# Local attention over key groups of 64, PSUM as eight freely placed banks, and a planner that charges mode changes

## The chip, the cores and the metric

The kernel runs on one core of one Trainium2 chip. Times are device microseconds of that core. Two kernels are compared by runs of the same rounds on the same chip. A run is "fast" or "slow", a slow one being over 1.5% above the fastest of its kernel. Engines are named as in the profile: PE is the matmul engine, PEld its weight loads, ACT the scalar engine, DVE the vector engine, POOL the third compute engine, SP the one that issues DMAs (in the kernel before all but one, of 0.9 KB).

## The reference, cut to what matters

```python
def _A_ref(x, wqkv, wo):               # S=2048 tokens, D=448, H=16 heads of 28
    W, dil = (8, 2)                    # each query sees 8 keys, every second position back
    ...
    logits = einsum('bhsd,bhswd->bhsw', q, kg) * scale
    attn = _softmax(where(mask, logits, -1e9))
    o = einsum('bhsw,bhswd->bhsd', attn, vg)
    return o.transpose(...).reshape(B, S, D) @ wo

x = x + ga * _A_ref(layernorm(x) * (1 + ca) + sa, A_wqkv, A_wo)
x = x + gb * _B_ref(layernorm(x) * (1 + cb) + sb, ...)     # an MLP 448 -> 1792 -> 448
```

The kernel keeps even and odd positions apart, so that the dilated window becomes 8 neighbours.

## The kernel before

A planner in Python adds tasks with a duration, an engine, dependencies and buffers. It simulates the engines and fixes the order of instructions on each engine and the buffer each task gets. The framework derives the semaphores afterwards. Two constants of the old planner: PSUM is `"L": 2` tiles of two banks and `"S": 4` tiles of one bank.

```python
def ps_big(shape, name):
    return Buf("L", lambda k: ps.tile(shape, FP32, name=name, tag=f"L{k}"), name)
def ps_one(shape, name, dtype=FP32):
    return Buf("S", lambda k: ps.tile(shape, dtype, name=name, tag=f"S{k}"), name)
```

Attention goes in 17 blocks of 121 queries against 128 keys. 16 logit matmuls use four row tiles of the array at a time; the denominators and the outputs use four column tiles. In the trace of this kernel the four logit matmuls of a round start within 11 ns, and the rounds of a group 52 to 66 ns apart (median 56).

```python
def lmm():
    for ft in range(4):
        for r in range(4):
            nc.tensor.matmul(lts[r // 2].t[:, r % 2, ft * EQ:(ft + 1) * EQ],
                             lhsT=kT[HP * r:HP * r + DH, ft, k0:k0 + BK],
                             rhs=qT[HP * r:HP * r + DH, ft, q0:q0 + EQ],
                             start=True, stop=True, tile_position=(HP * r, 0))
lm = add("PE", 0.45, lmm, ...)
...                                     # exp on ACT, mask on DVE
def dmm():
    for r in range(4):                  # denominators: 4 matmuls of 488 columns
        ...
    for ft in range(4):
        for r in range(4):              # outputs: 16 matmuls of 121 columns
            ...
add("PE", 0.62, dmm, ...)
```

The softmax here doesn't subtract the row's maximum and nothing guards it: scores larger than these inputs give would overflow.

Of the kernel before, what the change touches and what calls it, by code (L numbers as in the profile page):

```python
# [25 lines left out]
BQ, BK, EQ = 121, 128, 122  # L26
NBA = 17
WT = LEAD + SL + SEP + SL + 4
OTW = 9 * BQ
# [5 lines left out]
PASSES = (44,)  # L35
# [4 lines left out]
    (range(0, 5), [0]),  # L40
    (range(5, 9), [1, 2]),
    (range(9, 14), [3, 4]),
    (range(14, 17), [5, 6, 7]),
]
FILL_UNTIL, FILL_SHARE = 12.0, 1.0
ROOM = {"L": 2, "S": 4, "et": 3, "den": 4, "zh": 6, "yT": 3, "hm": 3, "vb": 3}
# [4 lines left out]
class Buf:  # L51


    def __init__(self, room, make, name=""):
        self.room, self.make, self.name, self.users, self._t = room, make, name, [], None
        self.slot = None
# [8 lines left out]
class Task:  # L65
    def __init__(self, n, eng, us, fn, bufs, rank_add, late, dense, port):
        self.n, self.eng, self.us, self.fn, self.bufs = n, eng, us, fn, bufs
        self.name = f"{eng} {fn.__qualname__.split('.')[-1]}:{fn.__code__.co_firstlineno}"
        self.rank_add, self.late, self.dense, self.port = rank_add, late, dense, port
        self.before, self.after = {}, []  # L70
        self.rank = 0.0
        self.fill = 0


class Planner:
# [6 lines left out]
    def add(self, eng, us, fn, reads=(), writes=(), bufs=(), after=(), order_after=(), rank_add=0.0, late=0.0, dense=1.0, port=False):  # L82
        t = Task(len(self.tasks), eng, us, fn, bufs, rank_add, late, dense, port or eng == "POOL")
# [59 lines left out]

    def forward(self):
# [6 lines left out]
        room = {r: [0.0] * n for r, n in ROOM.items()}  # L151
        users_left = {b: len(b.users) for t in self.tasks for b in t.bufs}
        free_at = {e: START for e in DRAIN}
        order = []
        now = START
        port = {"DVE": 0.0, "POOL": 0.0}
        while len(order) < len(self.tasks):
            started = False
            for e in ("PE", "DVE", "ACT", "POOL", "SP"):
                if free_at[e] > now:  # L160
                    continue
                best = None
                shared = e in port and port["DVE" if e == "POOL" else "POOL"] > now
                for t in ready[e]:
                    if ready_at[t] > now or (shared and t.port) or (best is not None and (t.rank, -t.n) < (best.rank, -best.n)):
                        continue
                    need = {}
                    for b in t.bufs:
                        if b.slot is None:
                            need[b.room] = need.get(b.room, 0) + 1  # L170
                    if all(sum(x <= now for x in room[r]) >= n for r, n in need.items()):
                        best = t
# [10 lines left out]
                for b in t.bufs:  # L183
                    if b.slot is None:
                        b.slot = min(range(ROOM[b.room]), key=lambda k: room[b.room][k])
                        room[b.room][b.slot] = 1e9
                end = now + t.us
                free_at[e] = end
# [3 lines left out]
                for b in t.bufs:  # L192
                    users_left[b] -= 1
                    if users_left[b] == 0:
                        room[b.room][b.slot] = done + SEM
# [10 lines left out]
            times = [v for v in free_at.values() if v > now] + [v for r in room.values() for v in r if now < v < 1e9]  # L206
            times += [ready_at[t] for e in ready for t in ready[e] if ready_at[t] > now]
# [24 lines left out]
    def plan(self):  # L232
        self.ranks()
        base = {t: t.rank for t in self.tasks}
        best, self.log = (None, None, 1e9), []
        for seed in PASSES:
            rnd = random.Random(seed)
            for t in self.tasks:
                t.rank = base[t] * (1.0 + (NOISE * rnd.gauss(0.0, 1.0) if seed else 0.0))
            for again in range(3):  # L240
                self.clear()
                order, span = self.forward()
# [3 lines left out]
                self.log.append((round(span, 1), round(cost, 1), seed))  # L246
                if cost < best[2]:
                    best = ([(t, t.fill) for t in order], {b: b.slot for t in order for b in t.bufs}, cost)
                self.backward()
        self.order, slots, self.span = best  # L250
        for b, k in slots.items():
            b.slot = k
# [9 lines left out]
def kernel(  # L262
# [28 lines left out]
    def ps_big(shape, name):  # L291
        return Buf("L", lambda k: ps.tile(shape, FP32, name=name, tag=f"L{k}"), name)

    def ps_one(shape, name, dtype=FP32):
        return Buf("S", lambda k: ps.tile(shape, dtype, name=name, tag=f"S{k}"), name)
# [22 lines left out]
    mask = cst.tile([128, 8, EQ], BF16, name="mask")  # L318
    ones_k = cst.tile([128, 3, HP], BF16, name="ones_k")
    neg_half = cst.tile([128, 4], FP32, name="neg_half")  # L320
    eps_col = cst.tile([128, 1], FP32, name="eps_col")
# [14 lines left out]
    NX1P = 8  # L336
    NZ, NY, NV = 4, 4, 3
# [110 lines left out]
    pool(0.1, lambda: nc.gpsimd.memset(neg_half[:], -0.5), ["neg_half"])  # L448
    pads = [(0, LEAD), (LEAD + SL, LEAD + SL + SEP), (LEAD + 2 * SL + SEP, WT)]
    for (a, b) in pads:  # L450
        for i, tl in enumerate((hT, kT, qT)):
            pool(0.12, lambda a=a, b=b, tl=tl: nc.gpsimd.memset(tl[:, :, a:b], 0.0), [f"pad{i}{a}"])
    PADK = [f"pad{i}{a}" for i in range(3) for (a, _) in pads]
    pool(0.9, lambda: nc.gpsimd.memset(mask[:], 1.0), ["mask"])
    pool(1.0, lambda: nc.gpsimd.affine_select(out=mask[:], in_=mask[:], pattern=[[0, 8], [1, EQ]],
                                              compare_op=ALU.is_ge, fill=0.0, base=WIN - 1, channel_multiplier=-1),
         ["mask"])
    pool(1.0, lambda: nc.gpsimd.affine_select(out=mask[:], in_=mask[:], pattern=[[0, 8], [-1, EQ]],
                                              compare_op=ALU.is_ge, fill=0.0, base=0, channel_multiplier=1), ["mask"])

    def consts():
# [4 lines left out]
        nc.gpsimd.memset(ones_k[64:64 + WIN - 1, 2, :], 0.0)  # L466
# [10 lines left out]
    pwm = ps_big([128, 2, 512], "pwm")  # L477
# [46 lines left out]
    P.wrote(add("PE", 0.3, c_cols, reads=["c_row", "c_tail", "one1"], bufs=[psc]), psc)  # L524
# [26 lines left out]
    def evac_h(kt, ptr, k, c0, n, eng, bs):  # L551
        kw = KE[kt]
# [11 lines left out]
    def front_ln(bs, on_act):  # L564
# [10 lines left out]
        for half, eng in enumerate(("DVE", "ACT")):  # L575
# [9 lines left out]
            P.wrote(add("PE", 0.13 * n, tr, reads=["ident", "ztail"] + [f"z{b % NZ}" for b in bs], bufs=[ptr]), ptr)  # L585
# [22 lines left out]
    def front_qk(bs, engs, bonus=0.0):  # L608
        n, c0 = 128 * len(bs), tok_col(bs[0])
        for m in range(8):  # L610
# [7 lines left out]
            P.wrote(add("PE", 4 * n / 2400 + 0.02, mm,  # L618
# [11 lines left out]
    def mods():  # L630
# [9 lines left out]
        P.wrote(add("PE", 1.1, mm, rank_add=150, reads=["silu_bc"] + [f"wmod2{i}{h}" for i in range(2) for h in "ab"] + ["wmod00", "wmod01"],  # L640
# [26 lines left out]
    def attention(b, tbl, prev_w1):  # L667
        q0 = LEAD + b * BQ
        k0 = q0 - (WIN - 1)
        tb = blocks_of(b * BQ - (WIN - 1), b * BQ + EQ)  # L670
        vbuf = Buf("vb", lambda k: vbufs[k], "vb")
        pv = ps_one([128, D], "pv")

        def vmm():
            for kt in range(KT):
                nc.tensor.matmul(pv.t[:], lhsT=hT[0:KE[kt], kt, k0:k0 + BK], rhs=Wv[0:KE[kt], kt, :],  # L676
                                 start=(kt == 0), stop=(kt == KT - 1))

        P.wrote(add("PE", 0.76, vmm, reads=["wva", "wvb", "Wv0"] + PADK + [f"h{kt}_{t}" for kt in range(KT) for t in tb], bufs=[pv, vbuf]), pv)
        P.wrote(add("ACT", 0.45, lambda: nc.scalar.copy(out=vbuf.t[:, :, 0:DH],  # L680
                                                        in_=pv.t[:].rearrange("p (h d) -> p h d", h=H)),
                    bufs=[pv, vbuf], reads=["vpad"]), vbuf)
        et = sb("et", [128, 4, 4, EQ], BF16, "et")
        lts = [ps_big([128, 2, 512], "lt") for _ in range(2)]

        def lmm():
            for ft in range(4):
                for r in range(4):
                    nc.tensor.matmul(lts[r // 2].t[:, r % 2, ft * EQ:(ft + 1) * EQ],  # L689
                                     lhsT=kT[HP * r:HP * r + DH, ft, k0:k0 + BK],  # L690
                                     rhs=qT[HP * r:HP * r + DH, ft, q0:q0 + EQ],
                                     start=True, stop=True, tile_position=(HP * r, 0))

        lm = add("PE", 0.45, lmm, dense=0.1, reads=PADK + [f"{s}{ft}_{t}" for s in "qk" for ft in range(4) for t in tb],
                 bufs=lts, order_after=prev_w1)
        P.wrote(lm, *lts)
        lt_mms.append(lm)
        for half in range(2):
            ex = add("ACT", 0.87, lambda half=half: nc.scalar.activation(  # L699
                out=et.t[:, 2 * half:2 * half + 2],  # L700
                in_=lts[half].t[:, :, 0:4 * EQ].rearrange("p r (ft c) -> p r ft c", ft=4),
                func=ACT.Exp, scale=float(DH) ** -0.5), bufs=[lts[half], et], writes=[(et, half)], order_after=[tbl])
            exps.append(ex)

            def msk(half=half):
                ev = et.t[:, 2 * half:2 * half + 2].rearrange("p r ft c -> p (r ft) c")
                nc.vector.tensor_tensor(out=ev, in0=ev, in1=mask[:], op=ALU.mult)  # L707

            add("DVE", 0.57, msk, port=True, bufs=[et], reads=["mask"], writes=[(et, half)])
        variant = 1 if b == 0 else (2 if b == 8 else 0)  # L710
        pd = ps_one([128, 4, EQ], "pd")
        po = ps_one([128, 4, BQ], "po")

        def dmm():
            for r in range(4):
                nc.tensor.matmul(pd.t[HP * r:HP * r + HP], lhsT=ones_k[:, variant, :], rhs=et.t[:, r],  # L716
                                 start=True, stop=True, tile_position=(0, HP * r))
            for ft in range(4):
# [202 lines left out]
```

## Time and profile before

The median is 188.36 us (four runs, 187.83 to 188.89).

The first lines and the chain of the page of the kernel before. The first number of an engine is its busy time in us, then its share of the span and its instructions.

```profile
span 186.7 us, 4230 instructions
## 1 busy us (share of the span) xinstructions
PE 176.1 (94%) x1709; PEld 107.9 (58%) x1709; DVE 131.2 (70%) x346; ACT 116.9 (63%) x170; POOL 49.3 (26%) x93
...
PE 81%; DVE 8%; ACT 4%; DMA 4%; issue 1%; DVEq 0%; ACTq 0%
```

PE is busy 94% and holds 81% of the chain that ended last. Its waits in the view of who waited for whom say the same. Columns are who waited, for whom, us in total, times, longest:

```profile
engine line waited for: us in total, times, longest us
PE pwm L481 <- DVE warm_w L378: 2.8, 1, 2.8
PE pq L615 <- ACT mod_rows L642: 0.8, 1, 0.8
PE ptr L582 <- DVE zbuf L511: 0.8, 1, 0.8
PE p L805 <- ACT hm L812: 0.5, 2, 0.2
...
```

After the start (2.8 us), PE waits under 4 us for others in the whole kernel. The timeline of the kernel before around one logit group (start, duration, engine, line, operation, count):

```profile
106.58 0.23 PEld L689 LDWEIGHTS <-kT 28*128 28x128 bf16 x16 [0.37 <-issue]
106.58 0.40 PE L689 MATMUL lt<-qT,kT 28*128 28x122 bf16 x16
...
106.91 0.49 PEld L676 LDWEIGHTS <-hT 128*128 128x128 bf16 x4
```

The group takes 0.33 us from its first weight load to the next group's. Matmuls overlap in the trace (those of 256 columns last 272 ns each and start 109 ns apart), so a sum of durations is no cost. I cost PE from start times instead: 512 columns start 215 ns apart, so a column takes 0.42 ns, and what lies between the last column of one matmul and the start of the next is a gap.

### The profile page before, as it was taken

Reading aid. Unit: us, or ns where it says so; the run is one execution under the profiler, and the core shown is the slowest. Engines: PE = TensorE matmul, PEld = TensorE weight load, DVE = VectorE, ACT = ScalarE, POOL = GpSimd, SP = SyncE. Lnnn points to the kernel's source line nnn. Section 1 sums busy time; section 2 is a strip of 40 time slices with the busy share of each in tenths; the row PEclk is TensorE's granted clock in tenths of the full one; section 3 lists DMA queues with packets and bytes.
Section 4 is the critical chain, followed back from the end, with each engine's and each line's share of the span. In section 5 each row is a group of like instructions: output and inputs, shape, how many; then the busy total and the mean of one; then the engine's idle time right before and its main releaser. Section 6 shows DMA issues by size and latency. Waiting matters only on the chain.

```text
span 186.7 us, 4230 instructions
## 1 busy us (share of the span) xinstructions
PE 176.1 (94%) x1709; PEld 107.9 (58%) x1709; DVE 131.2 (70%) x346; ACT 116.9 (63%) x170; POOL 49.3 (26%) x93
## 2 busy tenths in 40 slices
PE   4997888999999999999999999999999999999991
PEld 1574653453478546647864457478555666775750
DVE  3798799999994999787805799798259878211102
ACT  2269869767687998386587993784956473231230
POOL 7175001336501214325300052383003153000000
PEclk9999999999999999999999999999999999999999
DMA  5999599901101001002020100400401030210101
GB/s 175 306 351 271 170 236 281 297 6 30 28 4 28 4 0 30 18 14 77 4 56 0 53 4 0 103 2 4 86 4 49 2 81 0 56 40 12 49 0 51
DMA packets 19000, 13.91 MB, mean 75 GB/s; under 512 B 9246, under 2 KB 18403, under 8 KB 18980
## 3 DMA queue, kind: packets, MB, share of 16 engines
q1 hardware_dynamic: 18978, 13.64, 26.8%
q8 instruction: 13, 0.21, 0.5%
q14 instruction: 7, 0.06, 0.1%
q10 hardware_dynamic: 2, 0.00, 0.0%
HBM read 9.70 MB, written 1.84 MB: 62 GB/s over the span
## 4 chain that ended last, share of the span: by engine, by line
PE 81%; DVE 8%; ACT 4%; DMA 4%; issue 1%; DVEq 0%; ACTq 0%
PE p L805 26%; PE p L825 23%; PE pq L615 12%; PE pw L755 6%; PE pv L676 5%; PE pd L716 3%; DMA mod_bc<-mod_hbm 3%; PE lt L689 2%; DVE st_all L488 2%; PE po L720 2%; ACT hT L560 1%; PE pwm L481 1%; DVE et L707 1%; DMA mod_hbm<-mod_rows 1%; ACT hm L812 1%; ACT et L699 1%
## 5 line engine op out<-in xcount | busy, mean ns | idle before, releaser
L805 PE MATMUL p<-yT,w_s 128*128 128x256 bf16 x448 | 52.3, 272 | 0.5 <-ACT hm L812 0.5
L805 PEld LDWEIGHTS <-w_s 128*128 128x128 bf16 x448 | 43.5, 97 | 9.3 <-issue 1.1
L812 ACT ACTIVATE hm<-p 128x1024 bf16<-128x1024 f32 (+1 forms) x32 | 28.4, 916 | 30.2 <-PE p L805 30.2
L825 PE MATMUL p<-w_s,hm 128*128 128x448 bf16 x224 | 46.7, 353 | 0.0
L506 POOL TENSOR_TENSOR rs_all<-tv_all,neg_half 128x1 f32<-128x1 f32 (+1 forms) x35 | 22.2, 640 | 58.5 <-DVE tv_all L503 58.4
L699 ACT ACTIVATE et<-lt 128x976 bf16<-128x976 f32 x34 | 32.0, 987 | 3.6 <-PE lt L689 3.4
L615 PE MATMUL pq<-hT,Wqk 128*128 128x512 bf16 (+3 forms) x160 | 30.9, 337 | 2.0 <-ACT mod_rows L642 0.8
L707 DVE TENSOR_TENSOR et<-et,mask 128x976 bf16<-128x976 bf16 x34 | 23.0, 684 | 11.6 <-ACT et L699 11.3
L825 PEld LDWEIGHTS <-hm 128*128 128x128 bf16 x224 | 20.8, 98 | 17.6
L785 POOL TENSOR_TENSOR x1p_ring<-x_all,gbb_bc 128x448 f32<-128x448 bf16 x16 | 17.0, 1060 | 44.8 <-DVE x_all L759 26.4
L832 DVE TENSOR_TENSOR x_all<-p,x1p_ring 128x448 bf16<-128x448 f32 x16 | 9.9, 622 | 24.4 <-PE p L825 24.4
L615 PEld LDWEIGHTS <-Wqk 128*128 128x128 bf16 (+1 forms) x160 | 14.8, 97 | 14.4 <-issue 3.2
L488 DVE BATCH_NORM_STATS2 st_all<-x_all 128x6 f32<-128x448 bf16 x32 | 19.2, 617 | 1.1 <-DMA x_all<-in_A_x_dram 0.9
L726 ACT ACTIVATE lden<-pd 128x488 f32<-128x488 f32 x17 | 9.9, 583 | 12.1 <-PE pd L716 12.1
L676 PE MATMUL pv<-Wv,hT 128*128 128x448 bf16 x68 | 15.5, 352 | 0.3 <-DVE oT L735 0.2
L755 PE MATMUL pw<-wo_s,oT 128*128 128x448 bf16 x64 | 14.3, 353 | 0.1
L735 DVE SCALAR_TENSOR_TENSOR oT<-po,rden 128x484 bf16<-128x484 f32 x17 | 11.1, 654 | 1.1 <-ACT rden L728 1.0
L759 DVE TENSOR_TENSOR x_all<-pw,x_all 128x448 bf16<-128x448 f32 x16 | 9.8, 616 | 2.7 <-PE pw L755 1.9
L627 ACT CAST qT<-pq 128x512 bf16<-128x512 f32 (+1 forms) x15 | 7.5, 503 | 5.3 <-PE pq L615 5.1
L728 ACT ACTIVATE rden<-lden 128x488 f32<-128x488 f32 x17 | 10.4, 613 | 0.4
L676 PEld LDWEIGHTS <-hT 128*128 128x128 bf16 x68 | 6.4, 98 | 6.1 <-issue 0.7
L680 ACT CAST vbuf<-pv 128x448 bf16<-128x448 f32 x17 | 8.9, 540 | 1.3 <-PE pv L676 1.1
(82 smaller groups left out, 168.6 us busy)
## 6 DMA issues: line engine op xcount, KB each, us to landing
out_dram<-x_all SPq DMA_DIRECT2D x8, 224.0 KB, 2.1
w_s<-in_B_w_dram SPq DMA_DIRECT2D x2, 784.0 KB, 12.4
wmod<-in_w_mod_dram SPq DMA_DIRECT2D x2, 672.0 KB, 7.3
w_s<-in_B_w_dram SPq DMA_DIRECT2D x1, 1344.0 KB, 9.7
x_all<-in_A_x_dram SPq DMA_DIRECT2D x1, 896.0 KB, 8.4
wm_st<-in_w_mod_dram SPq DMA_DIRECT2D x1, 720.0 KB
wqk_st<-in_A_wqkv_dram SPq DMA_DIRECT2D x2, 339.0 KB, 5.4
x_all<-in_A_x_dram SPq DMA_DIRECT2D x2, 224.0 KB
```

The lines of the kernel that those rows point to most:

```text
L488: add("DVE", 0.53, lambda: nc.vector.bn_stats(out=st_all[:, sl, :], in_=src()), reads=key, writes=[f"st{sl}"])
L506: lambda: nc.gpsimd.tensor_tensor(out=rs_all[:, which, b0:b0 + n], in0=tv_all[:, which, b0:b0 + n], in1=neg_half[:, 0:n], op=ALU.pow),
L615: nc.tensor.matmul(pq.t[:], lhsT=wqk_m(kt, m), rhs=hT[0:KE[kt], kt, c0:c0 + n], start=(kt == 0), stop=(kt == KT - 1))
L676: nc.tensor.matmul(pv.t[:], lhsT=hT[0:KE[kt], kt, k0:k0 + BK], rhs=Wv[0:KE[kt], kt, :], start=(kt == 0), stop=(kt == KT - 1))
L699: ex = add("ACT", 0.87, lambda half=half: nc.scalar.activation(out=et.t[:, 2 * half:2 * half + 2], in_=lts[half].t[:, :, 0:4 * EQ].rearran ...
L707: nc.vector.tensor_tensor(out=ev, in0=ev, in1=mask[:], op=ALU.mult)
L735: nc.vector.scalar_tensor_tensor(out=oT[:, :, o0:o0 + BQ], in0=po.t[:], scalar=DEN_SCALE, in1=rden.t[:, :, 0:BQ], op0=ALU.mult, op1=ALU.mult)
L755: nc.tensor.matmul(pw.t[:], lhsT=oT[:, ft, c0:c0 + 128], rhs=wo_s[:, ft, :], start=(ft == 0), stop=(ft == 3))
L785: nc.gpsimd.tensor_tensor(out=x1p_ring[:, t % NX1P, :], in0=x_all[:, t, :], in1=gbb2_bc[:], op=ALU.add)
L805: nc.tensor.matmul(p1.t[:, f, :], lhsT=w1_s[0:kp, kt, (fq + f) * 128:(fq + f + 1) * 128], rhs=yT.t[0:kp, kt, :], start=(kt == 0), stop=(kt ...
L812: gl = add("ACT", 0.18 + nf * 0.183, lambda fq=fq, nf=nf, p1=p1: nc.scalar.activation(out=hm.t[:, fq:fq + nf, :], in_=p1.t[:, 0:nf, :], fu ...
L825: nc.tensor.matmul(p2.t[:], lhsT=hm.t[:, ft, bi * 128:(bi + 1) * 128], rhs=w2_s[:, ft, :], start=(ft == 0), stop=(ft == FT - 1))
```

## The change

The intent is a shorter PE stream. Queries go in 9 batches of 228: four key groups of 64, each with 57 queries. Eight array tiles are then meant to work at once (in the trace of the changed kernel the first eight matmuls of a logit burst start within 24 ns). Pieces of the diff:

```diff
-                nc.tensor.matmul(lts[r // 2].t[:, r % 2, ft * EQ:(ft + 1) * EQ], ... tile_position=(HP * r, 0))
-        lm = add("PE", 0.45, lmm, ...
+            for n in range(2):
+                for ft in range(4):
+                    for j in range(2):
+                        for r in range(4):       # 64 matmuls of 58 columns
+                            nc.tensor.matmul(lts[r // 2].t[WK * j:WK * j + WK, r % 2, c0:c0 + WE], ...
+                                             tile_position=(HP * r, WK * j))
+LMM, DMM = 0.35, 0.55                            # what the planner charges for the two bursts
+SWITCH, SAME = 0.095, 1.0                        # a mode change; a bonus for staying
...
-        return Buf("L", lambda k: ps.tile(shape, FP32, name=name, tag=f"L{k}"), name)
-        return Buf("S", lambda k: ps.tile(shape, dtype, name=name, tag=f"S{k}"), name)
+    pairs = [ps.tile([128, 2, 512], FP32, name=f"bank{2 * k}") for k in range(BANKS // 2)]
+        return Buf("P", lambda k: pairs[k // 2], name, banks=2)
+            flat = pairs[k // 2][:, k % 2, :]    # a one-bank buffer is half of a pair tile
...
-        for seed in PASSES:
+        for turn in range(TURNS):                # 60 turns from the best so far or from the base
...
-        pd = ps_one([128, 4, EQ], "pd")
-        po = ps_one([128, 4, BQ], "po")
+        pd = ps_big("pd")
+        po = ps_big("po")
```

Denominators become 8 matmuls of 464 columns, outputs 64 of 57. V needs 18 projections instead of 17, each from a copy of two key windows that DVE makes. ACT's Exp and Ln and DVE's mask work on fewer, wider pieces.

## The prediction

> **What bounds it now.** TensorE. The page shows PE 94% busy, and in the chain of waits PE holds 81%. From the start times of single matmuls, at 0.42 ns a column (512 columns start 216 ns apart), the array stands idle 25.9 of 186.7 us: about 10.6 before 30 us, 4.2 after the last matmul; between, some 11, of which about 6 are gaps of 0.06 to 0.15 us and 3 are waits. So from 30 us on, time falls only if the PE stream gets shorter. DVE (70%) and ACT (63%) bind only before about 45 us (windows: DVE 15.0 of 15 us from 30 to 45).
>
> **Switches.** Around 106 us the timeline shows 0.094 us lost on entering and on leaving a group: the last ordinary columns end at 106.487, the first logit weight load is at 106.581; logit columns end at 106.82, the next ordinary load is at 106.911. [...]
>
> **Attention on PE, per block of 121 queries.** 16 logit matmuls run as 4 rounds of 4 row tiles, 56 ns a round (122 columns), 0.235 us; denominators 0.216; outputs, 4 rounds, 0.23. With four switches 1.06 us; x17 = 18.0 us. V projection 0.757 x17.
>
> **After, per batch of 228 queries (9 batches).** Eight tiles work at once: logits 64 matmuls of 58 columns in 8 rounds, denominators 8 matmuls of 464 columns in one round (~0.2 us), outputs 8 rounds of 57 columns. [...] the modulation's single-column matmuls start 25.0 ns apart [...]. Pairs of load and matmul on different tiles start about 3.4 ns apart, so 8 take 27 ns. [...] I take 43: logits 0.35, denominators and outputs 0.55. With four switches 1.28 us x9 = 11.5 us. Saved 6.5 us; one V projection more (18 for 17) returns 0.76: **net 5.8 us, all on the critical chain.**
>
> **Other engines (mostly off the chain).** ACT: logit exp 34x0.987 plus ln and exp 17x(0.583+0.613) = 53.9 us becomes, at about 0.95 each, 34 us. DVE: masks 34 to 18, about -11 us; 18 window copies, about +5; divisions equal. This and free banks may recover about 1.5 us of waits, mainly from 20 to 60 us. The first attention needs 256 tokens, not 128, so little start-up is won.
>
> **Prediction:** 188.56 - 5.8 - 1.5 = about 181.3 us, range 178.5 to 185.5. Faster by over 2%: 0.80; within 2%: 0.17; slower by over 2%: 0.03.
>
> **What would show it.** (1) PE stays the chain at 80% or more, busy 93% or more. (2) A logit group's starts spread over 0.3 us, not 0.8. (3) About 36 gaps of 0.09 us instead of about 68. (4) Logit exp 18 at ~0.95; ACT busy near 98 us, DVE near 126.
>
> **What would make it wrong.** The sequencer not feeding 64 short pairs at 3.4 ns: the longest such burst in the trace has some 36 pairs. At 14 ns a pair logits and outputs would cost 0.9 us each, the gain would vanish. Or the window copies and bigger batches delaying the early phase, where DVE is already full[...]. If rounds come near 29 ns, about 179.

Its 43 ns a round was an estimate. It lies between two values of the kernel before: eight starts at 3.4 ns, 27 ns, and a round of four tiles with 122 columns, 56 ns. The 29 ns of its last line is an estimate too: 58 columns at 0.42 ns are 24.5 ns, and the round of 56 ns was 4.5 ns longer than its 122 columns (51.5 ns). The kernel before shows no eight tiles at once; the changed one does (in its trace the first eight matmuls of a logit burst start within 24 ns).

## The result, and the profile after

The changed kernel takes 202.56 us (four runs, 202.28 to 203.47) against 188.36. The ratio is 1.0764, with a 95% interval of 1.0732 to 1.0796. Ratios here are the mean time of one kernel's fast runs over that of the other's of the same rounds, so they are not quite the ratio of the medians; the profiled run is left out where enough other fast runs remain.

The page of the changed kernel, the lines that answer to those above:

```profile
span 200.7 us, 5448 instructions
## 1 busy us (share of the span) xinstructions
PE 177.2 (88%) x2323; PEld 112.6 (56%) x2333; DVE 122.0 (61%) x348; ACT 102.8 (51%) x139; POOL 48.4 (24%) x97
...
PE 74%; DVE 13%; ACT 8%; issue 3%; DVEq 0%; ACTq 0%
```

ACT and DVE did lose work, as predicted, and PE has more idle time. Its waits:

```profile
PE bank L562 <- DVE zbuf L461: 2.8, 1, 2.8
PE bank L696 <- ACT vbuf L768: 2.2, 2, 1.1
PE bank L941 <- DVE x_all L948: 1.6, 3, 0.7
PE bank L562 <- ACT hT L641: 1.2, 1, 1.2
PE bank L870 <- ACT vbuf L768: 1.2, 1, 1.2
...
PE bank L941 <- DVE x_all L874: 1.0, 2, 0.7
PE bank L829 <- issue: 0.9, 1, 0.9
```

Some of these make no sense as data dependencies. L696 (the q and k projection) has nothing to take from L768, a copy of V. The second MLP product (L941) needs nothing that L874, the residual add after attention, makes. They can only be waits for a PSUM place. The timeline of the changed kernel shows a logit group and such a wait:

```profile
110.95 0.59 PEld L789 LDWEIGHTS <-kT 28*64 28x64 bf16 x64 [0.37 <-issue]
110.95 0.70 PE L789 MATMUL bank<-qT,kT 28*64 28x58 bf16 x64
...
111.58 1.06 PEld L941 LDWEIGHTS <-hm 128*128 128x128 bf16 x7
111.59 1.31 PE L941 MATMUL bank<-w_s,hm 128*128 128x448 bf16 x6
...
112.93 0.62 DVE L948 TENSOR_TENSOR x_all<-bank,x1p_ring 128x448 bf16<-128x448 f32 x1 [1.08 <-PE bank L941]
...
113.61 0.73 PE L941 MATMUL bank<-w_s,hm 128*128 128x448 bf16 x3 [0.71 <-DVE x_all L948]
```

Two things are to be seen. The logit group takes 0.63 us to the next load, for 228 queries; before it was 0.33 for 121. And at 113.61 PE stands still 0.71 us until DVE has read a finished product. In the built program, that matmul writes the second bank of its pair tile and the DVE instruction reads the first bank. They share the tile and not one byte.

I then went through every wait of the built programs and looked up the instruction that each semaphore count stands for. In the kernel before, no wait of PE, ACT or DVE on another engine is for an instruction that touched only the other bank of a shared tile. In the changed one 42 waits of PE (on ACT and DVE), 27 of DVE on PE and 14 of ACT on PE are of that kind. 13 gaps of PE over 0.15 us end at such a wait alone; beyond the columns of the matmul before, they sum to 6.9 us (leaving out L696, of which 9 matmul records are missing). With L696, and with gaps that end at such a wait among others, it is 22 gaps and at most 12.8 us. What the 41 waits of DVE and ACT delay comes on top.

A ledger of the PE engine, worked out from the start times in each trace, in us. Nine missing L696 records (0.21 us each) are moved back from waits to columns:

```
                             before   changed
columns streaming             160.8     159.9
mode changes (gaps)        6.2 (63)  4.1 (36)
waits and holes                 6.1      21.7
start, warm-up, tail, small    13.6      15.1
span                          186.7     200.7
```

Nearly the whole loss is in the waits: 15.6 us more. The last line grew by 1.5 us, and columns and mode changes together fell by only 3.0 us. The clock is not the cause: the changed kernel's profiled run was granted 0.83 from 20 to 30 us and 0.991 on average, but its run at a granted clock of 1.0 took 202.28 us all the same.

### The profile page after: what moved, and what is told of

Its sections match the earlier page's. It is cut to its first block, busy times and chain, and to the rows that moved or that the text cites. A ratio compares the mean times of both kernels' runs of the same rounds, so it can differ in the third digit from the quotient of the medians.

```text
span 200.7 us, 5448 instructions
## 1 busy us (share of the span) xinstructions
PE 177.2 (88%) x2323; PEld 112.6 (56%) x2333; DVE 122.0 (61%) x348; ACT 102.8 (51%) x139; POOL 48.4 (24%) x97
## 4 chain that ended last, share of the span: by engine, by line
PE 74%; DVE 13%; ACT 8%; issue 3%; DVEq 0%; ACTq 0%
PE bank L920 24%; PE bank L941 20%; PE bank L696 13%; PE bank L870 5%; PE bank L764 4%; DVE x_all L874 2%; ACT vbuf L768 2%; DVE x_all L948 2%; DVE st_all L569 2%; ACT qT L708 2%; ACT hT L641 2%; PE bank L663 2%; PE bank L562 2%; PE bank L789 2%; PE bank L829 1%
## 5 line engine op out<-in xcount | busy, mean ns | idle before, releaser
L920 PE MATMUL bank<-yT,w_s 128*128 128x256 bf16 x448 | 52.1, 272 | 1.3 <-ACT hm L927 1.1
L941 PE MATMUL bank<-w_s,hm 128*128 128x448 bf16 x224 | 47.8, 352 | 3.3 <-DVE x_all L948 1.6
L927 ACT ACTIVATE hm<-bank 128x1024 bf16<-128x1024 f32 (+1 forms) x32 | 28.6, 915 | 40.4 <-PE bank L920 39.6
L696 PE MATMUL bank<-hT,Wqk 128*128 128x512 bf16 (+3 forms) x151 | 31.6, 349 | 5.1 <-ACT vbuf L768 2.2
L948 DVE TENSOR_TENSOR x_all<-bank,x1p_ring 128x448 bf16<-128x448 f32 x16 | 9.8, 617 | 41.7 <-PE bank L941 34.2
L941 PEld LDWEIGHTS <-hm 128*128 128x128 bf16 x224 | 21.3, 97 | 21.7 <-issue 4.6
L696 PEld LDWEIGHTS <-Wqk 128*128 128x128 bf16 (+1 forms) x160 | 16.1, 102 | 17.2 <-issue 5.9
L799 ACT ACTIVATE et<-bank 128x928 bf16<-128x928 f32 x18 | 16.0, 940 | 3.5 <-PE bank L789 3.3
L764 PE MATMUL bank<-Wv,hw 128*128 128x448 bf16 x72 | 16.1, 352 | 0.7 <-ACT vbuf L768 0.5
L768 ACT CAST vbuf<-bank 128x448 bf16<-128x448 f32 x18 | 9.4, 534 | 13.1 <-PE bank L764 8.4
L870 PE MATMUL bank<-wo_s,oT 128*128 128x448 bf16 x64 | 14.2, 352 | 1.6 <-ACT vbuf L768 1.2
L807 DVE TENSOR_TENSOR et<-et,mask 128x928 bf16<-128x928 bf16 x18 | 11.1, 636 | 4.4 <-ACT et L799 4.4
L854 DVE TENSOR_TENSOR oT<-bank,lden 128x456 bf16<-128x456 f32 x18 | 10.8, 619 | 4.1 <-ACT lden L844 4.1
L874 DVE TENSOR_TENSOR x_all<-bank,x_all 128x448 bf16<-128x448 f32 x16 | 9.7, 614 | 5.1 <-PE bank L870 3.5
```

Of the source, the lines that this page charges most:

```text
L696: nc.tensor.matmul(pq.t[:], lhsT=wqk_m(kt, m), rhs=hT[0:KE[kt], kt, c0:c0 + n], start=(kt == 0), stop=(kt == KT - 1))
L764: nc.tensor.matmul(pv.t[:], lhsT=hw.t[0:KE[kt], kt].rearrange("p j k -> p (j k)"), rhs=Wv[0:KE[kt], kt, :], start=(kt == 0), stop=(kt == K ...
L799: ex = add("ACT", 0.825, lambda half=half: nc.scalar.activation(out=et.t[:, 2 * half:2 * half + 2].rearrange("p r n ft c -> p r (n ft c)") ...
L870: nc.tensor.matmul(pw.t[:], lhsT=oT[:, ft, c0:c0 + 128], rhs=wo_s[:, ft, :], start=(ft == 0), stop=(ft == 3))
L874: add("DVE", 0.54, lambda: nc.vector.tensor_tensor(out=x_all[:, t, :], in0=pw.t[:], in1=x_all[:, t, :], op=ALU.add), bufs=[pw], writes=[f" ...
L920: nc.tensor.matmul(p1.t[:, f // 2, f % 2 * 256:f % 2 * 256 + 256], lhsT=w1_s[0:kp, kt, (fq + f) * 128:(fq + f + 1) * 128], rhs=yT.t[0:kp, ...
```

## The experiments

Theory A: the two banks of a pair tile are one thing for the dependency tracking, so neighbours wait for each other. Theory B: the planner charges too little for the bursts (0.35 and 0.55 us) and its order goes wrong. Theory C: the new attention itself is what costs. The first four runs tell them apart. "Before" was 188.07 us in their rounds.

### Control: the spanning ACT instructions cut in two

With eight one-bank tiles, no instruction of this program spans two banks any more. So the control first cuts those that do and keeps the pair tiles. The instruction order on PE is the same as in the changed kernel.

```diff
-            ex = add("ACT", 0.825, lambda half=half: nc.scalar.activation(out=et.t[:, 2*half:2*half+2]..., in_=lts[half].t[:, :, 0:2 * SBE], ...
+            ex = add("ACT", 0.825, lambda half=half: [nc.scalar.activation(out=et.t[:, 2*half+i]..., in_=lts[half].t[:, i, 0:2 * SBE], ...) for i in range(2)], ...
```

> Control for the next run: the changed kernel with the same order and the same pair tiles, but every ScalarE instruction that spans both banks of a pair (logit Exp, Ln, GELU) cut in two, one per bank. Theory A (the two banks of a pair are one tile to the dependency tracking, so instructions wait for the neighbouring bank's users): the shared tiles are still there, so it stays slow, 201 to 206 us; ScalarE busy grows from 103 to about 111 us. Theory B (the planner's too low charges for the attention bursts upset its order): also 201 to 206 us. If it fell below 198, cutting the ScalarE work itself would be a cause.

Measured: 203.2 us, ratio 1.080. Cutting by itself changes the time by less than 1 us. (ACT's busy time rose to 105.7 us only, not to the 111 expected.)

### Eight one-bank tiles, the same order

```diff
-    pairs = [ps.tile([128, 2, 512], FP32, name=f"bank{2 * k}") for k in range(BANKS // 2)]
+    tiles8 = [ps.tile([128, 512], FP32, name=f"bank{k}") for k in range(BANKS)]
+    class Two:                           # pair k: item [p, i, ...] is tiles8[k + i][p, ...]
+        ...
+    pairs = [Two(2 * k) for k in range(BANKS // 2)]
```

> The same cut instructions and the same planned order and bank numbers, but eight tiles of one bank instead of four of two. Theory A: the 42 TensorE waits, and the 41 of ScalarE and VectorE on TensorE, that name only the neighbouring bank's user vanish; of the roughly 15 us of TensorE waits more than before, at least 9 go; 184 to 192 us. Theory B: the order is unchanged and so are its errors: 200 to 206 us.

Measured: 189.9 us, ratio 1.0041 (0.9935 to 1.0146); one of its four runs was slow and is left out of the ratio. That is 13.3 us less than the control by the medians, 13.8 without the slow run, with the same planned order and bank numbers. No wait for a neighbouring bank is left in the built program. The waits of PE in this run:

```profile
PE bank L572 <- DVE zbuf L471: 2.8, 1, 2.8
PE bank L839 <- issue: 1.7, 1, 1.7
PE bank L673 <- DVE zbuf L602: 1.1, 1, 1.1
PE bank L572 <- DVE mod_col L636: 0.8, 1, 0.8
...
```

All waits of the second MLP product, of the q and k projection (the former L696) and of the output projection are gone. The same place of the order as above, in this run's timeline (L958 is the former L948, L951 the former L941, L799 the logits):

```profile
99.87 0.62 DVE L958 TENSOR_TENSOR x_all<-bank,x1p_ring 128x448 bf16<-128x448 f32 x1 [3.99 <-PE bank L951]
100.45 0.70 PE L799 MATMUL bank<-qT,kT 28*64 28x58 bf16 x64
101.08 1.69 PE L951 MATMUL bank<-w_s,hm 128*128 128x448 bf16 x8
...
102.70 0.70 PE L799 MATMUL bank<-qT,kT 28*64 28x58 bf16 x64
103.34 2.07 PE L951 MATMUL bank<-w_s,hm 128*128 128x448 bf16 x10
```

The ten matmuls that stopped after six now run through. Theory A holds, and B doesn't explain the loss.

### Eight tiles, and the bursts charged as measured

```diff
-LMM, DMM = 0.35, 0.55
+LMM, DMM = 0.54, 0.69
```

> As the eight-tile run, with the planner told what the trace shows for the bursts: logits 0.54 us instead of 0.35, denominators and outputs 0.69 instead of 0.55. Theory A: a small further change, within 2 us of the eight-tile run (183 to 191 us). Theory B: most of the loss goes here and not in the eight-tile run, so over 6 us faster than that.

Measured: 187.4 us, ratio 0.9928 (0.9841 to 1.0015). One of its four runs was slow too. By the means of the fast runs (189.2 and 187.0 us) theory B is worth about 2 us, and the two intervals overlap, so even this is not clear of the noise. It is far from the 6 us that theory B needed. The 0.69 was itself a little low: by start times a denominator and output burst takes 0.78 us.

### The old attention with the new PSUM and planner

The kernel before, with this change's pair tiles and planner, and nothing of the new attention.

```diff
-ROOM = {"L": 2, "S": 4, ...}
+BANKS = 8
+    pairs = [ps.tile([128, 2, 512], FP32, name=f"bank{2 * k}") for k in range(BANKS // 2)]
-        lm = add("PE", 0.45, lmm, ...
+        lm = add("PE", 0.235, lmm, mode="32x128", ...   # and SWITCH on entering and leaving
```

> The kernel before with its own attention, but with this change's PSUM (four pair tiles, freely placed) and its planner (mode charge, 60 turns). Theory A: slower than before although the attention is the old one, 193 to 204 us, with TensorE waits of over 10 us after 30 us. Rival C (the new attention's short matmuls and bigger batches are what costs): within 2% of before, 187 to 192 us (the planner's own estimate for this order is 3 us above that for the order of before).

Measured: 214.1 us, ratio 1.1376. It is well outside the expected range, in the direction of theory A: here the pair tiles hurt even more. Theory C falls as the main cause: without the new attention the loss is larger.

### The same with eight one-bank tiles

```diff
-    pairs = [ps.tile([128, 2, 512], ...)]
+    tiles8 = [ps.tile([128, 512], FP32, name=f"bank{k}") for k in range(BANKS)]   # and Exp, GELU cut in two
```

> The kernel with the old attention of the earlier pair-tile run (214 us), with eight one-bank tiles and the spanning ScalarE instructions cut in two; planned order and bank numbers the same. If the shared pair tiles are the cause there too, it falls by 18 to 25 us to 188 to 196 us (the planner's own estimate is 190, and other runs with eight tiles stand some 5 us above theirs). If the old attention under this planner is what is slow, it stays above 205.

Measured: 192.3 us, ratio 1.0207 (1.0157 to 1.0257). Unsharing the banks gives back 21.8 us of the old attention's 214.1.

### The planner's part alone

Old attention, old PSUM rooms; mode charge, bonus and 60 turns.

```diff
-PASSES = (44,)
+SEED, TURNS = 44, 60
+SWITCH, SAME = 0.095, 1.0
```

> The kernel before with only the planner's part of the change: mode charge, bonus for staying in a mode, 60 turns; old attention, old PSUM with two fixed two-bank and four one-bank tiles. The planner's own estimate is 1.5 us above that of before's order. Expect within 2%: 187 to 191 us. A gain of over 2% would say that the search itself is worth something; a loss of over 2% that the planner's charge hurts by itself.

Measured: 191.7 us, ratio 1.0174 (1.012 to 1.0228): just above the range that I gave. The search and the charge gain nothing here. Why this order is 3 us worse than the old one's was not followed up.

### Each logit burst issued twice

This asks what limits a burst: the rate at which instructions come, or the rounds of the array. The result stays correct, since the second pass writes the same values.

```diff
-            for n in range(2):
+            for n in (0, 1, 0, 1):
```

> The eight-tile kernel with measured burst costs, same planned order, but each batch's 64 logit matmuls are issued twice in a row (the second pass writes the same values). Theory F (a burst past its first 30 or so pairs is fed at about 8.3 ns a pair): each of the 9 bursts gets 64 x 8.3 = 0.53 us longer, the span 3.5 to 5 us (the first bursts partly hidden in waits), and the starts of the second pass stand 8.3 ns apart. Rival R (the array's rounds of 58 columns bind, 29 ns for 8 pairs): 0.23 us a burst, 1.5 to 2.1 us in all, starts 3.6 ns apart on average.

The timeline of one doubled burst:

```profile
54.90 1.13 PEld L799 LDWEIGHTS <-kT 28*64 28x64 bf16 x128 [0.37 <-issue]
54.90 1.24 PE L799 MATMUL bank<-qT,kT 28*64 28x58 bf16 x128
```

By start times, single bursts of 64 spread over 0.497 us and the four undisturbed ones of the nine doubled bursts over 1.029: the second 64 add 0.53 us, 8.3 ns each. So theory F holds for the bursts and rival R falls. In the changed kernel the first 32 pairs of load and matmul start in rounds of eight, 3.4 ns apart within a round, and all within 0.14 us; after a pause of 0.1 us every further pair takes 8.3 ns. What sets this rate was not tested.

The measured time, however, is 204.3 us (ratio 1.0817), some 17 us more and not 5, so the forecast for the whole kernel failed. Beside the 4.8 us of the second passes, the trace shows holes inside bursts, about 11 us in all, for which the profile names no releaser. It also shows a clock that was granted at 0.964 on average in the profiled run: 0.50 from 22 to 26 us and 0.62 from 42 to 46. (The two longest holes are those from 17.70 to 21.63 and from 34.97 to 39.11 us.) The same run's PE timeline:

```profile
34.05 0.92 PE L799 MATMUL bank<-qT,kT 28*64 28x58 bf16 x90
39.11 0.57 PE L799 MATMUL bank<-qT,kT 28*64 28x58 bf16 x38 [4.14 <-issue]
```

I set the holes of all traces beside the records of the DMA queue q8, which the page marks as instruction. Its packets are 16,384 bytes, and there are 13, 18 and 23 of them for the 3,418, 4,666 and 5,818 loads and matmuls of the kernel before, the changed one and this run. That is one packet for every 263, 259 and 253 of them, or some 130 pairs, an estimate from these counts. From the first to the last, packets start 12.5 us apart on average in the kernel before and 9.7 in the changed one. Yet in all 14 holes of 0.4 to 4.3 us inside attention bursts that end at no wait (eight traces with the new attention; the four traces with the old one have none), the end of the hole comes 1.26 to 1.59 us after the end of such a packet (for example packet to 37.81, hole to 39.11; in the changed kernel packet to 21.34, hole from 21.70 to 22.78; in the eight-tile kernel with measured costs packets to 28.38 and 35.14, holes to 29.64 and 36.55). That instructions came late is the guess from this timing; no run took the packets away, so it is not shown.

### No instruction cut: pair tiles for the two-bank buffers alone

The eight-tile runs also release banks in finer pieces. This run does without that: two fixed pair tiles for two-bank buffers, four one-bank tiles for the rest, nothing cut. Burst costs are as measured, the seed is 21 and the turns 120.

```diff
+BANKS, BIG = 8, 4
-    pairs = [ps.tile([128, 2, 512], ...) for k in range(BANKS // 2)]
+    pairs = [ps.tile([128, 2, 512], ...) for k in range(BIG // 2)]
+    tiles1 = {k: ps.tile([128, 512], FP32, name=f"bank{k}") for k in range(BIG, BANKS)}
-            for k in range(0, BANKS, b.banks):
+            for k in range(0, BIG, 2) if b.banks == 2 else range(BIG, BANKS):
```

> The changed kernel with no instruction cut: the two-bank buffers (logits, denominators, outputs, first MLP product) keep two fixed pair tiles, and all one-bank buffers get four one-bank tiles of their own, so no two one-bank buffers share a tile; burst costs as measured, another seed. If false waits between one-bank neighbours are the cause (and not the finer release that cutting instructions gives in the eight-tile run), it runs at 185 to 190 us with TensorE waits after 30 us under 6 us. If the finer release was what helped, it stays above 196.

Measured: 187.2 us, ratio 0.9976 (0.9923 to 1.0029), correct, on the page:

```profile
span 184.8 us, 5457 instructions
PE 174.0 (94%) x2333; PEld 111.3 (60%) x2333; DVE 125.9 (68%) x348; ACT 102.6 (55%) x139; POOL 48.7 (26%) x97
```

PE is back at 94% with the uncut instructions. So the waits end without the finer release as well. (The order and the burst costs differ from the changed kernel's here; no run has the pair tiles with this order, so how much the finer release gave in the eight-tile runs is not shown.) Only 3 of PE's waits are still for the other bank of a tile (po halves read by two DVE instructions).

### A version that beats both, and its luck

Eight tiles, measured burst costs, the cut ACT pieces charged at their measured distance (Exp 0.437, Ln 0.45, GELU 0.476 us), two other charges raised a little (window copy 0.24, second Exp of the denominators 0.98), 120 turns, seed 11; then two more seeds.

```diff
-SEED, TURNS = 44, 60
+SEED, TURNS = 11, 120
-LMM, DMM = 0.35, 0.55
+LMM, DMM = 0.54, 0.69
```

> Candidate to beat both: eight tiles, burst costs as measured, the cut ScalarE instructions charged as the eight-tile trace shows them (Exp pieces 0.437 us start to start, Ln 0.45, GELU 0.476), 120 turns of search with another seed. The planner's estimate is 1.2 us below that of the order with measured bursts only, which ran at 187.4. Expect 184 to 187.5 us, ratio to before 0.98 to 0.995; TensorE waits after 30 us under 3 us.

Measured: 185.3 us (six fast runs, 184.43 to 186.23), ratio 0.9818 (0.9776 to 0.986). It beats both kernels. The old one it beats by 1.8%: the interval lies below 1, but reaches across 2% on both sides, so a gain of 2% is neither shown nor ruled out. Its page:

```profile
span 183.7 us, 5515 instructions
PE 174.5 (95%) x2326; PEld 113.0 (61%) x2334; DVE 121.9 (66%) x348; ACT 108.3 (59%) x190; POOL 48.3 (26%) x97
```

> The calibrated eight-tile kernel with another search seed; the planner's estimate is the same (179.1 us), so what differs is only luck of the order: 184 to 187.5 us, ratio to before 0.98 to 0.995.

> As the previous run with a third seed (planner's estimate 179.2 us): 184 to 187.5 us. Single holes of about 1 us inside the attention bursts next to instruction packets, if they fall in, cost 1 to 2 us more.

Measured: 191.4 us and 191.4 us by median, but four of six runs of each are slow. The two fast ones average 188.6 and 188.0 us, with ratios 1.0014 and 0.9985. Both missed the range by either measure. The slow runs have mean granted clocks of 0.973 to 0.991; the only runs at 1.0 took 187.2 and 186.6 us. These two orders seem more prone to stretches in which the clock falls, and their traces hold holes of 1.4 to 1.5 us after an instruction packet as well. The planner's estimate, equal for all three seeds within 0.1 us, sees neither. Which feature of an order brings the clock down was not tested.

## Why the prediction was wrong

**What bounds the kernel** was read rightly: PE, with almost no waits after 30 us (2.8 us in the kernel before). The new waits cost nearly their full length: 15.6 us more of waits and holes, 14.0 us more of span.

**The step that failed is "This and free banks may recover about 1.5 us of waits".** The sign was wrong. Waits and holes grew by 15.6 us. I took "eight freely placed banks" for more freedom. In the planner they are; but the waits come from the tiles, and the change had made one tile of each two banks. Undoing that took 13.3 us away (203.2 to 189.9) at the same planned order, perhaps with some help of the finer release; in the old attention it took 21.8 us away (214.1 to 192.3). The evidence was there before any run: the built program lists its waits, and 42 waits of PE on a neighbour's bank could have been counted.

**The size of the PE saving** was wrong too: "I take 43: logits 0.35, denominators and outputs 0.55". The trace shows 0.54 and 0.78. With four mode changes of 0.094, a batch costs 1.70 us and not 1.28; nine cost 15.3 us. Against 18.0 before, that saves 2.7, and less one V projection 1.9 us, where I wrote 5.8; the ledger, which counts shared mode changes once, shows 3.0. The prediction had named this risk ("the sequencer not feeding 64 short pairs at 3.4 ns"). I had taken 43 ns for a round of eight. The first four rounds of a logit burst do start some 40 ns apart (at 0, 54, 87 and 119 ns), but after the pause the rate is 8.3 ns a pair, 66 a round: neither my 3.4 nor the 14 at which the gain would have vanished.

**The signs.** (1) failed: PE is 74% of the chain and 88% busy. (2) A logit burst's starts spread over 0.50 us, between the two values. (3) held: 36 gaps at mode changes instead of 63 (I had said 68). (4) held: 18 Exp of 0.940 us; ACT 102.8 us busy (98 predicted), DVE 122.0 (126 predicted). The gap at a mode change was 0.09 us before and after, from the last column to the next weight load (medians of 0.092 and 0.094 us by start times).

**The early phase**, which I had named as a risk, isn't what cost: waits before 30 us grew from 3.4 to 6.4 us by the trace, and those after 30 us from 2.8 to 17.2 (the missing records, all after 30 us by their place, would take 1.9 off that). A fall of the clock was seen as well (0.83 from 20 to 30 us), but is not what cost either, as the run at 1.0 shows (202.28 us).

With the tiles unshared and the costs set right, the change is worth 1.8% at best and about nothing with the other orders tried (0.9928, 0.9976, 1.0014, 0.9985). The attention by itself does save something: with eight tiles, seed 44 and 60 turns, the new one stands at 1.0041 and the old one at 1.0207, some 3 us apart, as in the ledger. The orders differ, so this is an indication only. The new planner's order takes about as much away (1.0174 and 1.0207 with the old attention).

## What to carry to other kernels

A planner that places buffers must use the same unit as the machinery that derives the waits: if two buffers share a declared tile they may wait for each other, however disjoint their bytes (here 42 waits of PE; eight tiles took 13.3 us of 203 away). Before a change of allocation runs, count in the built program which waits are for an instruction that touches other bytes. When matmuls are made shorter and more numerous, cost them by the rate at which a long burst of them starts, measured beyond the first 32 pairs or so, and not by the first few (here 8.3 ns a pair against 3.4).
